# Fourth and sixth chunk of batches 1 to 7: computed key pairs ahead of fetched ones

## Chip, core and metric

One core of a Trainium2 chip. The metric is the device time of one execution in microseconds (us); the kernel before takes 2296.9 us (median of three runs, 2296.57 to 2297.46).

## What is computed

For 8 batches of 3200 rows, an attention without softmax and a gated unit behind it:

```
scores = (1/S) * z @ z.T          # z: 3200 x 64
attn   = relu(scores) ** 2        # symmetric
x      = u * (attn @ v)           # u, v: 3200 x 256
gate   = sigmoid(causal conv of x over 5 rows)
out    = ((x @ w_val) * gate) @ w_out
```

Every product is made of three matmuls of fp32r parts (high by high, high by low, low by high).

## The kernel before

**Tiling.** The 25 tiles of 128 rows of a batch are taken in seven chunks of queries (4, 4, 4, 4, 3, 3, 3 tiles; in the last batch 4, 4, 4, 4, 4, 3, 2). I call them c0 to c6 here, so the fourth and sixth are c3 and c5. Against each chunk stand 13 pairs of key tiles, numbered 0 to 12; the last "pair" is a single tile. One chunk with one pair is a step; all steps stand in one list (`steps`), sorted by batch, chunk and `place`, the pair's position in its chunk. I write c3 p5 for the step at place 5 of c3.

**Three kinds of pairs.** `attn` is symmetric, so a block whose keys belong to an earlier chunk was already computed, with the roles exchanged. `turn` (L419, L429) transposes such a block on DVE, `keep` (L441) stores it in DRAM, `m_fetch` (L450, L456) loads it again into one of four `m` buffers. Such a pair is *fetched* (`mirrored` in the code). Other pairs are *computed*: `scores` on PE into PSUM, Relu and Square on ACT (L501, L502). Two pairs are mixed: `halves` (half of a diagonal block is fetched) and `split` (one of two tiles is fetched). Each kind ends alike: a cast on ACT makes the high part `ah` (L504), a subtraction on DVE the low part `al` (L510; L491 for mixed pairs).

**What PE does in a step.** `attend` multiplies `ah`, `al` of the step's pair by `v`. Scores are made three steps ahead (`AHEAD`). If the pair three steps ahead is not fetched, the step runs in *half rows*: `attend` (L338, through `side_by_side`) cuts each matmul in two of 64 rows that run beside each other, and the scores (contraction 64) go between its two parts. Otherwise the step runs in *whole rows*: `attend_whole` (L544), with no scores. The same choice is made for the work that is tied to a chunk's places: `project` or `project_whole` (L700) of the chunk before the last at p0, and `value` or `value_whole` (L652) of the last chunk at p5.

**What sets the order.** Python loops write each engine's order out by hand. `todo` holds the rest of the work by step: `BEHIND` the gated unit of the chunk before (at p9 `gate_value(1)` on DVE, L664; at p10 `gate_value_high(1)` on ACT, L668; at p11 `gate_value_low(1)` on DVE, L673, whose result `gvl` the projection at the next p0 reads), `u_prep` (L563), `x_low` (L601), and `z_order` (L226), two ACT copies that put a chunk's queries into block order in the single buffer `zq`. In a step, PE's work comes first, then `todo`, then `weights_of` for the pair three ahead; the subtraction and turn of a step p11 wait until `gated` (L574), which needs the chunk's last matmul.

Of the kernel before, what the change touches and what calls it, by code (L numbers as in the profile page):

```python
# [13 lines left out]
BLK = 32  # L14
# [3 lines left out]
def attn_glu_kernel(  # L18
# [30 lines left out]
    B, S, D = u.shape  # L49
# [8 lines left out]
    n_chunks = -(-NT // 4)  # L58
# [4 lines left out]
    i = even.index(base) if extra < n_chunks else None  # L63
# [4 lines left out]
    all_firsts = [[sum(sz[:i]) for i in range(n_chunks)] for sz in all_sizes]  # L68
# [146 lines left out]

    zq = {}

    def has_copy(b, c):

        return c < n_chunks - 1 and b > 0  # L220

    def z_order(b, c, x):
# [11 lines left out]
    pairs = [(k, min(2, NT - k)) for k in range(0, NT, 2)]  # L234
    NP = len(pairs)

    def two_pairs(b, c):

        first = all_firsts[b][c]
        return all_sizes[b][c] == 4 and first % 2 == 0 and first < NT // 2 + 2 and (b > 0 or c > 1)  # L240

    def own(b, c, x):
        return all_firsts[b][c] // 2 + x

    place = {}
    for b in range(B):
        for c in range(n_chunks):
            order = list(range(NP))
            if two_pairs(b, c):
                order.append(order.pop(own(b, c, 1)))  # L250
            if b == B - 1 and c == n_chunks - 1:
                new = [i for i in order if sum(pairs[i]) > all_firsts[b][c]]
                order = new + [i for i in order if i not in new]
            for p, i in enumerate(order):
                place[b, c, i] = p
# [74 lines left out]
    def side_by_side(upper, lower):  # L330


        ins = None
        for i in range(max(len(upper), len(lower))):
            for r, mms in zip(rows, (upper, lower)):
                if i < len(mms):
                    out_, st, mv, first, last = mms[i]
                    ins = nc.tensor.matmul(out_, st[r], mv[r], start=first, stop=last)  # L338
        return ins
# [24 lines left out]
    def scores(b, c, i, terms=range(3)):  # L364
        k, n = pairs[i]
        w = all_sizes[b][c] * P
        if (b, c, i) not in st_:
            st_[b, c, i] = ps.tile([P, 2, 512], F32, name="s", bufs=2)
        s = st_[b, c, i]

        q = zt[b, c][:, :, :w].rearrange("p x (t a r) -> p x a t r", t=all_sizes[b][c], r=BLK)
        if has_copy(b, c):
            q = zq[b, c][:, :, :w].rearrange("p x (a y) -> p x a y", a=P // BLK)
        if halves(b, c, i):
            q, w = q[:, :, :, 2 * BLK :] if has_copy(b, c) else q[:, :, :, 2:], w // 2
        a = P // BLK
        sides = []
        for j in range(2):

            one_tile = n == 1 or split(b, c, i)  # L380
            g, t = all_homes[b][k + (n - 1 if one_tile else j)]
            ks = slice(t * P, (t + 1) * P)
            qs = slice(j * (a // 2), (j + 1) * (a // 2)) if one_tile else slice(0, a)
            kk = zt[b, g]
            mms = []
            for m in terms:
                kp, qp = ((0, 1), (1, 0), (0, 0))[m]
                mms.append((s[:, j, : w // 2 if one_tile else w], kk[:, kp, ks], q[:, qp, qs], m == 0, m == 2))
            sides.append(mms)
        side_by_side(*sides)  # L390
# [8 lines left out]
    def halves(b, c, i):  # L399
        return two_pairs(b, c) and i == own(b, c, 1)  # L400

    def split(b, c, i):

        (j, g, *_), *more = runs(b, i)
        return bool(more) and more[0][1] == c and keeps(b, g, c) and (b, c) != (B - 1, n_chunks - 1)

    def mirrored(b, c, i):
        return all(keeps(b, all_homes[b][t][0], c) for t in range(pairs[i][0], sum(pairs[i])))
# [326 lines left out]
    AHEAD = 3  # L735
    FETCH = 3
    VALUE = 5

    def project_at(b, c):

        return 2 if (b, c) == (0, 2) else 0
# [5 lines left out]
    def at_step(s, fn, *args, first=False):  # L747
        work = todo.setdefault(min(s, END), [])
        work.insert(0 if first else len(work), (fn, args))

    def start(b, c):
        return (b * n_chunks + c) * NP
# [29 lines left out]
    for b in range(B):  # L782
        for c in range(n_chunks):
            s0 = start(b, c)
            nxt = s0 + NP
            for h in range(DH):
                for part in range(2):
                    at_step(max(s0 + U_LOAD[b > 0][c], 2) + 2 * h + part, u_load, b, c, h, part)
            if (b, c) != LAST:
                for r, fn, args in BEHIND:  # L790
                    at_step(nxt + r, fn, b, c, *args)
                for x in range(DH):
                    at_step(nxt + project_at(*steps[nxt][:2]) + 1 + x, out_copy_before, b, c, x)
            at_step(max(s0 + U_PREP[b > 0][c], 6), u_prep, b, c)

            met = start(b, 0) + all_firsts[b][c] // 2 - AHEAD
            if has_copy(b, c):
                for x in range(2):
                    at_step(s0 - (5 if c == 0 else 3), z_order, b, c, x)
            if b == 0:  # L800
                met -= c == 1
                at_step(met - 5, z_load, b, c)
                early = 1 if c == 0 else 0
                at_step(met - 3 - early, z_turn, b, c)
                at_step(met - 2 - early, z_high, b, c)
                at_step(met - 1 - early - (c >= 2), z_low, b, c)
            else:
                s1 = Z_FROM[b][c] + start(b - 1, 4)
                at_step(s1, z_load, b, c)
                late = 1 if b == 1 else 0  # L810
                at_step(s1 + late + 3, z_turn, b, c)
                at_step(s1 + late + 4, z_high, b, c)
                at_step(s1 + late + 5, z_low, b, c)
            for i in range(NP):
                if mirrored(b, c, i) or halves(b, c, i) or split(b, c, i):
                    at_step(s0 + place[b, c, i] - AHEAD - FETCH, m_fetch, b, c, i, first=True)
        if b == 0:
            for i in range(NP):
                at_step(i - 3, v_high, b, i)
                at_step(i - 2 if i else -3, v_low, b, i)  # L820
            for g in range(n_chunks):
                at_step(all_firsts[b][g] // 2 - 5, v_load, b, g)
        else:
            s, kept_at, loads = start(b - 1, 1) + 2, {}, []
            for g in range(n_chunks):
                load_at = s - 5
                for t in range(0, all_sizes[b][g], 2):
                    at_step(s, v_make_high, b, g, t)
                    at_step(s + 1, v_make_low, b, g, t)
                    at_step(s + 2, v_keep, b, g, t)  # L830
                    for k in range(t, min(t + 2, all_sizes[b][g])):
                        kept_at[(all_firsts[b][g] + k) // 2] = s + 5
                    s += 5
                loads.append((load_at, v_load, b, g))
                s += 2
            for i in range(NP):
                at_step(max(start(b, 0) - NP + i + 2, kept_at[i]), v_fetch, b, i)
            for load in loads:
                at_step(*load)
# [8 lines left out]
    with tc.manual_schedule():  # L848
        zeros = sb.tile([P, CW], F32R, name="zeros", tag="gvl", bufs=1)
        nc.vector.memset(f32(zeros), 0.0)  # L850
        for s in range(min(todo), END + 1):
            b, c, i = steps[s] if s >= 0 else (0, 0, 0)
# [51 lines left out]
            if s == END:  # L904
# [4 lines left out]
                b, c = LAST  # L909
# [66 lines left out]
```

## Time and profile before

| | |
|---|---|
| median of three runs | 2296.9 us |
| the profiled execution's own time | 2296.48 us |
| its span in the trace | 2294.7 us |
| PE matmul busy | 2287.3 us, 100% of the span |
| PE weight load busy | 88% |
| DVE busy | 79% |
| ACT busy | 77% |
| DMA engines | 76.3% on the main queue, 203 GB/s |
| granted TensorE clock | full in all 40 slices of the page |

Busy times of PE overlap (matmuls are pipelined), so a matmul's price is read from the distance between starts, not from its duration. Times in rows are us from the span's start. The batches 1 to 6 repeat each other closely, so batch 3 is shown: c2 runs from 961.6, c3 from 1007.2, c4 from 1051.5, c5 from 1086.0 and c6 from 1119.5.

### The profile page before, as it was taken

How to read it: one execution, taken by the hardware profiler on the slowest of the kernel's cores; microseconds unless marked ns; L12 is line 12 of the kernel's file. 1: busy time of each engine (PE TensorE's matmuls, PEld its weight loads, DVE VectorE, ACT ScalarE, POOL GpSimd, SP SyncE). 2: the span in 40 equal slices, each digit the busy share in tenths (PEclk: the TensorE clock that was granted, in tenths of full speed). 3: DMA queues.
4: the chain of work that ended last, by engine and by line, in shares of the span. 5: the costliest groups of instructions: out<-in, count | busy, mean ns of one | idle time of the engine just before them, and what ended most of it. 6: DMA issues, size and time to landing. Idle time of an engine off the chain costs nothing.

```text
span 2294.7 us, 47249 instructions
## 1 busy us (share of the span) xinstructions
PE 2287.3 (100%) x18629; PEld 2009.2 (88%) x18629; DVE 1817.6 (79%) x2391; ACT 1777.5 (77%) x2402; POOL 54.7 (2%) x108
## 2 busy tenths in 40 slices
PE   9999999999999999999999999999999999999999
PEld 8788988889888998889988899888998889988889
DVE  8777788788878878788788887888877887778776
ACT  8988788776888768887688776887768876687765
POOL 0000000000000000000000000000000000000000
PEclk9999999999999999999999999999999999999999
DMA  6265797778977889688987789878897788966653
GB/s 133 65 157 149 211 265 201 200 205 247 255 182 202 215 242 252 170 213 221 241 238 192 197 227 248 224 189 213 235 232 213 203 223 228 256 172 170 187 164 91
DMA packets 688576, 466.39 MB, mean 203 GB/s; under 512 B 355297, under 2 KB 639201, under 8 KB 688353
## 3 DMA queue, kind: packets, MB, share of 16 engines
q1 hardware_dynamic: 687296, 463.23, 76.3%
q8 instruction: 146, 2.39, 0.4%
q14 instruction: 78, 0.63, 0.1%
q10 hardware_dynamic: 1056, 0.13, 0.0%
HBM read 251.73 MB, written 211.48 MB: 202 GB/s over the span
## 4 chain that ended last, share of the span: by engine, by line
PE 94%; ACT 2%; SPq 1%; DVE 1%; issue 1%; DMA 1%; ACTq 0%; DVEq 0%
PE acc L338 44%; PE acc L544 28%; PE s L338 10%; PE misc L338 6%; PE misc L700 4%; PE misc L652 1%; SPq L166 1%; ACT a L502 1%; ACT a L501 1%; ACT ah L504 0%; SPq L280 0%; DMA m<-mir 0%; DVE gvl L673 0%; DVE al L510 0%; DMA u_raw<-in_u_dram 0%
## 5 line engine op out<-in xcount | busy, mean ns | idle before, releaser
L338 PE MATMUL acc<-ah,v_hl 64*128 64x512 f32 (+1 forms) x6632 | 1074.3, 375 | 0.6 <-DVE v_hl L296 0.6
L338 PEld LDWEIGHTS acc<-ah,v_hl 64*128 64x128 f32 x6632 | 623.3, 184 | 110.6 <-issue 11.8
L544 PE MATMUL acc<-ah,v_hl 128*128 128x384 f32 (+2 forms) x2284 | 638.6, 355 | 0.1
L338 PE MATMUL acc<-al,v_hl 64*128 64x512 f32 (+1 forms) x3316 | 628.2, 374 | 0.0
L510 DVE TENSOR_TENSOR al<-a,ah 128x1024 fp32r<-128x1024 f32 (+3 forms) x388 | 424.1, 1093 | 222.8 <-ACT ah L504 215.0
L501 ACT ACTIVATE a<-s 128x1024 f32<-128x1024 f32 (+3 forms) x388 | 357.2, 921 | 152.2 <-PE s L338 149.1
L544 PEld LDWEIGHTS acc<-ah,v_hl 128*128 128x128 f32 x2284 | 416.8, 188 | 47.4 <-ACT a L474 6.4
L510 DVE TENSOR_TENSOR al<-m,ah 128x768 fp32r<-128x768 f32 (+2 forms) x303 | 307.8, 1023 | 121.9 <-ACT ah L504 121.2
L544 PE MATMUL acc<-al,v_hl 128*128 128x384 f32 (+2 forms) x1142 | 402.2, 352 | 0.1
L502 ACT ACTIVATE a<-a 128x1024 f32<-128x1024 f32 (+3 forms) x388 | 372.3, 960 | 12.3
L504 ACT CAST ah<-m 128x768 fp32r<-128x768 f32 (+2 forms) x303 | 267.1, 892 | 146.7 <-DMA m<-mir 111.0
L338 PEld LDWEIGHTS acc<-al,v_hl 64*128 64x128 f32 x3316 | 314.2, 184 | 45.4
L504 ACT CAST ah<-a 128x1024 fp32r<-128x1024 f32 (+3 forms) x350 | 333.6, 953 | 11.1
L419 DVE STREAM_TRANSPOSE turned<-a 128x1024 f32<-128x1024 f32 (+3 forms) x318 | 320.0, 1011 | 22.3 <-DMA mir<-turned 21.2
L615 DVE SCALAR_TENSOR_TENSOR gate<-x,cw,gate 128x512 f32<-128x512 f32 (+2 forms) x448 | 303.3, 677 | 4.5 <-ACT gate L613 0.3
L338 PE MATMUL s<-zq,zhl 64*128 64x512 f32 (+3 forms) x2052 | 259.8, 356 | 0.0
L544 PEld LDWEIGHTS acc<-al,v_hl 128*128 128x128 f32 x1142 | 214.8, 188 | 15.1 <-DVE al L510 0.3
L338 PEld LDWEIGHTS s<-zq,zhl 64*128 64x128 f32 x2052 | 185.4, 184 | 29.5
L620 ACT ACTIVATE gate<-gate 128x512 f32<-128x512 f32 (+2 forms) x112 | 65.4, 584 | 43.3 <-DVE gate L615 43.1
L574 DVE TENSOR_TENSOR x<-acc,ut 128x512 f32<-128x512 f32 (+2 forms) x112 | 67.4, 629 | 39.4 <-PE acc L338 25.2
L668 ACT CAST gvh<-gv 128x512 fp32r<-128x512 f32 (+2 forms) x112 | 64.0, 572 | 26.6 <-DVE gv L664 26.4
L304 ACT CAST v_made<-v_raw 128x512 fp32r<-128x512 f32 x97 | 55.9, 576 | 36.5 <-DMA v_kept<-v_made 35.4
(116 smaller groups left out, 2018.2 us busy)
## 6 DMA issues: line engine op xcount, KB each, us to landing
m<-mir SPq DMA_DIRECT2D x191, 384.0 KB, 4.9
mir<-turned SPq DMA_DIRECT2D x340, 192.0 KB, 3.9
mir<-turned SPq DMA_DIRECT2D x188, 256.0 KB, 4.3
m<-mir SPq DMA_DIRECT2D x94, 512.0 KB, 6.0
v_hl<-v_kept SPq DMA_DIRECT2D x84, 512.0 KB, 6.7
v_kept<-v_made SPq DMA_DIRECT2D x71, 512.0 KB, 5.4
u_raw<-in_u_dram SPq DMA_DIRECT2D x264, 64.0 KB, 3.3
out_dram<-ob SPq DMA_DIRECT2D x33, 512.0 KB, 4.0
```

Of the source, the lines that this page charges most:

```text
L338: ins = nc.tensor.matmul(out_, st[r], mv[r], start=first, stop=last)
L419: nc.vector.transpose(into[:, t : t + m], a[:, j * w : (j + m) * w].rearrange("p (t m x) -> p t m x", t=m, x=BLK))
L501: nc.scalar.activation(a.rearrange("p (j x) -> p j x", j=2), s[:, :, :each], AF.Relu, scale=scale)
L502: nc.scalar.activation(a, a, AF.Square)
L504: nc.scalar.copy(hi, a)
L510: nc.vector.tensor_tensor(lo, a, f32(hi), op=ALU.subtract)
L544: nc.tensor.matmul(out_, st, mv, start=first, stop=last)
L574: nc.vector.tensor_tensor(x[:, h, HALO : HALO + w], accs[b, c][h][:, :w], ut[b, c][:, h, :w], op=ALU.mult)
L615: nc.vector.scalar_tensor_tensor(g, tap, cw[:, h, k : k + 1], g, op0=ALU.mult, op1=ALU.add)
L620: nc.scalar.activation(g, g, AF.Sigmoid)
L668: nc.scalar.copy(gvs[b, c][0][:, e, :w], gv_[b, c, e][:, :w])
L700: nc.tensor.matmul(out_, st, mv, start=first, stop=last)
```

## The change

For c3 of batches 1 to 7 and c5 of batches 1 to 6 (`new_first`), the places are given anew: computed pairs first (in c5 the split pair last of them), fetched pairs behind. c3 was 0 1 2 3 4 5 | 6 8 9 10 11 12 7 and is 6 8 9 10 11 12 7 | 0 1 2 3 4 5; c5 was 0 to 8 | 9 10 11 12 and is 10 11 12 9 | 0 to 8. Since c4 and c6 begin with fetched pairs, and c2 and c4 end with computed ones, the stretches run together. Three things follow. The queries of c3 and c5 are needed in order earlier, so `z_order` moves from three steps ahead of the chunk to five. The single `zq` is then no longer the previous chunk's at that chunk's last place, so its last pair reads the queries unordered. And the fetch of c3's `halves` pair is made one step later, after its store.

```diff
-    def has_copy(b, c):
-
+    def has_copy(b, c, i=None):
+        if i is not None and new_first(b, c + 1) and place[b, c, i] == NP - 1:
+            return False
         return c < n_chunks - 1 and b > 0
...
+    def new_first(b, c):
+        return b > 0 and c % 2 == 1 and 1 < c < n_chunks - (2 if b == B - 1 else 1)
...
+            if new_first(b, c):
+                new = [i for i in order if sum(pairs[i]) > all_firsts[b][c]]
+                new.sort(key=lambda i: pairs[i][0] < all_firsts[b][c])
+                order = new + [i for i in order if i not in new]
...
-        if has_copy(b, c):
+        if has_copy(b, c, i):
             q = zq[b, c][:, :, :w].rearrange("p x (a y) -> p x a y", a=P // BLK)
...
-                    at_step(s0 - (5 if c == 0 else 3), z_order, b, c, x)
+                    at_step(s0 - (5 if c == 0 or new_first(b, c) else 3), z_order, b, c, x)
...
-                    at_step(s0 + place[b, c, i] - AHEAD - FETCH, m_fetch, b, c, i, first=True)
+                    at_step(s0 + place[b, c, i] - AHEAD - FETCH + (new_first(b, c) and halves(b, c, i)), m_fetch, b, c, i, first=True)
```

**PE, from c2 p9 to c2 p10 of batch 3**, before (v_hl10 and v_hl11 are the pairs 10 and 11; s is a block of scores):

```order
L338 MATMUL acc1_13281<-al_13626,v_hl10_11979 128x512
L338 MATMUL acc0_13280<-ah_13625,v_hl10_11979 128x512
L338 MATMUL acc1_13281<-ah_13625,v_hl10_11979 128x512
L544 MATMUL acc0_13280<-ah_13677,v_hl11_12120 128x512
L544 MATMUL acc0_13280<-al_13678,v_hl11_12120 128x512
L544 MATMUL acc0_13280<-ah_13677,v_hl11_12120 128x512 x2
```

And in the change, where the same step goes on in half rows, with scores of c3 (zhl3 and zq) between its parts:

```order
L350 MATMUL acc0_13330<-ah_13675,v_hl10_12029 128x512
L350 MATMUL acc1_13331<-ah_13675,v_hl10_12029 128x512
L350 MATMUL acc0_13330<-ah_13725,v_hl11_12170 128x512
L350 MATMUL acc1_13331<-ah_13725,v_hl11_12170 128x512
L350 MATMUL acc0_13330<-al_13726,v_hl11_12170 128x512
...
L350 MATMUL s_13848<-zq_13770,zhl3_11109 128x512 x6
L350 MATMUL acc1_13331<-ah_13725,v_hl11_12170 128x512
```

The switch to whole rows at c2 p10 is gone; it comes after c3 p3 now.

**ACT, from c4 p8 to c4 p10 of batch 3**, before (a<-s is the Relu of a computed pair, ah<-m the cast of a fetched one, zq<-zhl5 is `z_order` of c5, gvh is `gate_value_high(1)`):

```order
L620 ACTIVATE gate_22108<-gate_22108 128x512
L501 ACTIVATE a_22430<-s_22397 128x768
L502 ACTIVATE a_22430<-a_22430 128x768
L504 CAST ah_22428<-a_22430 128x768
L501 ACTIVATE a_22475<-s_22449 128x384
L502 ACTIVATE a_22475<-a_22475 128x384
L504 CAST ah_22473<-a_22475 128x384
L668 CAST gvh_22315<-gv_22471 128x512
L226 CAST zq_22496<-zhl5_19240 128x384 x2
L504 CAST ah_22506<-m_22368 128x4x2x96
```

And in the change:

```order
L632 ACTIVATE gate_22214<-gate_22214 128x512
L229 CAST zq_22525<-zhl5_19340 128x384 x2
L513 ACTIVATE a_22535<-s_22501 128x768
L514 ACTIVATE a_22535<-a_22535 128x768
L516 CAST ah_22533<-a_22535 128x768
L513 ACTIVATE a_22578<-s_22554 128x384
L514 ACTIVATE a_22578<-a_22578 128x384
L516 CAST ah_22576<-a_22578 128x384
L680 CAST gvh_22421<-gv_22574 128x512
L513 ACTIVATE a_22628<-s_22596 128x768
L514 ACTIVATE a_22628<-a_22628 128x768
L516 CAST ah_22626<-a_22628 128x768
```

The two copies stand ahead of the Relu of place 11, and where one cast of a fetched pair followed `gvh`, three instructions of c5's first computed pair follow it.

## Rows read from the trace of the kernel before

**Rows 1.** PE's waits in the whole span: total us, times, longest us

```profile
PE misc L700 <- DVE gvl L673: 0.3, 1, 0.3
```

**Rows 2.** PE timeline, half to whole, c2 p9/p10: start, us, line, tiles, shapes, count

```profile
999.96 0.39 PE L338 MATMUL acc<-ah,v_hl 64*128 64x512 f32 x2
1000.28 0.50 PE L544 MATMUL acc<-ah,v_hl 128*128 128x512 f32 x1
...
1003.38 0.39 PE L544 MATMUL acc<-al,v_hl 128*128 128x512 f32 x1
```

**Rows 3.** PE timeline, twelve whole-row matmuls amid a stretch, c3 p1 to p2

```profile
1014.67 0.61 PE L544 MATMUL acc<-ah,v_hl 128*128 128x512 f32 x2
...
1017.39 0.61 PE L544 MATMUL acc<-ah,v_hl 128*128 128x512 f32 x2
```

**Rows 4.** PE timeline, whole to half, c3 p2/p3

```profile
1018.07 0.39 PE L544 MATMUL acc<-ah,v_hl 128*128 128x512 f32 x1
1018.38 0.50 PE L338 MATMUL acc<-ah,v_hl 64*128 64x512 f32 x2
...
1019.88 0.86 PE L338 MATMUL s<-zq,zhl 64*128 64x512 f32 x6
```

**Rows 5.** PE timeline, whole to half at 384 columns, c5 p5/p6

```profile
1101.73 0.33 PE L652 MATMUL misc<-xh,w_val_lo 128*128 128x384 f32 x1
...
1103.63 0.34 PE L652 MATMUL misc<-xh,w_val_hi 128*128 128x384 f32 x1
1103.90 0.44 PE L338 MATMUL acc<-ah,v_hl 64*128 64x384 f32 x2
```

**Rows 6.** PE timeline, projection in whole rows at c5 p0

```profile
1086.04 0.28 PE L700 MATMUL misc<-w_out_hi,gvl 128*128 128x256 f32 x1
...
1086.63 0.28 PE L700 MATMUL misc<-w_out_hi,gvh 128*128 128x256 f32 x1
1086.98 0.39 PE L700 MATMUL misc<-w_out_hi,gvl 128*128 128x256 f32 x1
```

**Rows 7.** PE timeline, projection in half rows at c1 p0: nine pairs of matmuls

```profile
916.17 0.28 PE L338 MATMUL misc<-w_out_hi,gvl 64*128 64x256 f32 x2
...
917.24 0.39 PE L338 MATMUL s<-zq,zhl 64*128 64x512 f32 x2
```

**Rows 8.** ACT timeline, c4 p8 to c5 p0

```profile
1078.12 0.80 ACT L501 ACTIVATE a<-s 128x768 f32<-128x768 f32 x1
...
1083.15 0.62 ACT L668 CAST gvh<-gv 128x512 fp32r<-128x512 f32 x1 [1.00 <-DVE gv L664]
1083.67 0.93 ACT L226 CAST zq<-zhl 128x384 fp32r<-128x384 f32 x2
1084.50 0.83 ACT L504 CAST ah<-m 128x768 fp32r<-128x768 f32 x1
```

**Rows 9.** DVE timeline, c4 p8 to c5 p0

```profile
1080.69 0.96 DVE L510 TENSOR_TENSOR al<-a,ah 128x768 fp32r<-128x768 f32 x1 [0.56 <-ACT ah L504]
...
1082.46 0.65 DVE L664 TENSOR_TENSOR gv<-misc,gate 128x512 f32<-128x512 f32 x1
...
1085.37 0.96 DVE L510 TENSOR_TENSOR al<-m,ah 128x768 fp32r<-128x768 f32 x1 [0.71 <-ACT ah L504]
1086.24 0.68 DVE L673 TENSOR_TENSOR gvl<-gv,gvh 128x512 fp32r<-128x512 f32 x1
```

**Rows 10.** DVE timeline, the `gvl` that the projection at c3 p0 reads

```profile
1005.03 0.69 DVE L673 TENSOR_TENSOR gvl<-gv,gvh 128x512 fp32r<-128x512 f32 x1
```

**Rows 11.** DVE timeline in c5 p1: `x_low` and, after `u_prep`, the next subtraction

```profile
1091.58 0.95 DVE L601 TENSOR_TENSOR xl<-x,xh 128x768 fp32r<-128x768 f32 x1
...
1093.35 0.92 DVE L510 TENSOR_TENSOR al<-m,ah 128x768 fp32r<-128x768 f32 x1
```

**Rows 12.** Windows, c6: length, busy us by engine (PE first), clock, DMA share, GB/s

```profile
1119.51:1153.03 33.52, 33.52 (x266) 32.86 (x266) 26.84 (x44) 20.50 (x33) 0.98 (x2) 1.00 1.04 270
```

**Rows 13.** The page's DMA issues, fetches of 384 KB: count, KB, median us

```profile
m<-mir SPq DMA_DIRECT2D x191, 384.0 KB, 4.9
```

More of the change, by code (lines that the diff above doesn't have):

```diff
@@ L371, in scores @@
         q = zt[b, c][:, :, :w].rearrange("p x (t a r) -> p x a t r", t=all_sizes[b][c], r=BLK)
-        if has_copy(b, c):
+        if has_copy(b, c, i):
             q = zq[b, c][:, :, :w].rearrange("p x (a y) -> p x a y", a=P // BLK)
         if halves(b, c, i):
-            q, w = q[:, :, :, 2 * BLK :] if has_copy(b, c) else q[:, :, :, 2:], w // 2
+            q, w = q[:, :, :, 2 * BLK :] if has_copy(b, c, i) else q[:, :, :, 2:], w // 2
         a = P // BLK
```

## The prediction

> **What bounds the kernel now.** I read the list of PE's waits first, then PE's timeline by the distance of starts, and only then the engines that feed PE. The page has PE busy for 100% of the span, and past batch 0 the list of waits names nothing but a projection that waits 0.3 us for `gvl` [rows 1]; batch 3 shows such a gap at c5 p0, between 1086.63 and 1086.98 [rows 6]. So the kernel is PE's issue, step after step, and a gain has to come out of the distances between PE's starts. In a stretch of whole rows, twelve matmuls of 512 columns take 2.72 us, 0.227 each [rows 3]; at 384 columns eleven take 1.90 us, 0.173 each [rows 5]. A pair of half-row matmuls costs the same as one whole-row matmul. What stands out are the switches between the two: the starts around them are further apart.
>
> **What a switch costs.** Half to whole at 512 columns: the last pair starts 0.32 us before the first whole-row matmul, 0.09 over the pitch, and the next 13 take 3.10 us instead of 2.95 [rows 2, 3]: 0.24. Whole to half: 0.31 at the border, 0.08 over, then six pairs in 1.50 us instead of 1.36 [rows 4]: 0.22. At 384 columns the border is 0.27 against 0.173, 0.10 over [rows 5]; I take the tail of 0.12 that it has from the 512 rows, so 0.22 each way. A stretch of whole rows costs its two switches: 0.46 us at 512, 0.44 at 384.
>
> **What the change removes.** In each of batches 1 to 7 the stretch at the border of c2 and c3 melts into that of c3 and c4 (512 columns), and in batches 1 to 6 that of c4 and c5 into that of c5 and c6 (384). The kinds of pairs are as many as before, so half and whole steps are too. Gone are 7 x 0.46 + 6 x 0.44 = 5.9 us, all of it on PE's path.
>
> **What it moves on PE.** The projections at c3 p0 and c5 p0 go from whole to half rows. Five whole-row matmuls take 0.59 us [rows 6], nine half-row pairs 1.07 [rows 7]: 0.118 against 0.119. But half rows put a score group amid the projection, where the row widths change twice more; I price that between 0 and 0.1 us (a switch's border), 0.05 each, 13 times 0.05 = 0.7 us back. The value matmuls of c3 go from half to whole at the same pitch: nothing. The unordered scores of a chunk's last pair (13 of them) show in no row; they are between 0 and 0.1 us as well, and I take nothing, since the same number of columns streams. PE alone would gain 5.2 us.
>
> **What it moves on the others.** The two `z_order` copies go ahead of the Relu of c4 place 11, and three instructions of a computed pair now stand between `gvh` and the subtraction that precedes `gvl`. This is the place that decides, because PE already waits there. Before: Relu of place 11 at 1078.12, its subtraction at 1080.69, `gv` at 1082.46, `gvh` at 1083.15, the copies at 1083.67, the cast of c5's first pair at 1084.50, its subtraction at 1085.37, `gvl` from 1086.24 to 1086.92 [rows 8, 9]. No engine has slack in this chain: ACT goes from one cast to the next until place 12, and DVE takes `gv` behind the turn of place 11. In the change the copies push the Relu, and everything to `gvh`, by their 0.83 us (1083.67 to 1084.50): `gvh` at 1083.98. After it (0.52) comes a Relu, and from a Relu to its subtraction it is 2.57 us (1078.12 to 1080.69), so that starts at 1087.07, and `gvl` 0.87 behind it at 1087.94: 1.70 later than before.
>
> The projection starts later too: c4 p10 to p12 now carry scores, two groups of three pairs at 0.173 and one half as wide, 1.3 us, less the switch of 0.22 that goes: 1.1 us. So PE waits about 0.6 longer than before, on top of the 0.35 - 0.12 = 0.23 us at the seventh matmul [rows 6]. In half rows the seventh pair is again the first to read the late part. Six times 0.55 (between 0.5 and 0.6) is 3.3 us given back. Bounds: at best the old wait goes too (0.3 each, 1.9 gained), at worst the whole 1.70 counts, as if the projection started no later (10 us); I stay with the chain, whose every link has a row.
>
> At c3 p0 the same chain has room: `gvl` starts at 1005.03 [rows 10], done 0.69 later, 1.5 us ahead of the projection, with which c3 starts at 1007.2. It moves by some 2.6 (the same three ACT instructions at 1024 elements, with the copies now ahead of a place that is a single tile), the projection by 1.8: 0.7 are left. Nothing is charged.
>
> The fetches of c5 move four places back, so twenty fetched pairs follow each other to c6 p10. A buffer comes back every four steps, 4 x 12 x 0.173 = 8.3 us, against 4.9 for the landing [rows 13], 0.83 for the cast and 0.96 for the subtraction [rows 8, 9]: 6.7. Hidden, with 1.6 us to spare a turn. SP's queue has the store of c5's turned blocks, which waits for the turn of c5's third pair, ahead of the fetch for p7; by the line of DVE's work under the second rival that is some 7 us into c5, and p7 comes some 20 us into it.
>
> **Sum.** -5.9 + 0.7 + 3.3 = -1.9. The profiled execution took 2296.48 us, which would make 2294.6; the median of the runs is 0.4 above it, so I predict **2295.0**. A measurement of this kernel can tell about 0.2%, 4.6 us; the forecast lies inside that.
>
> **Rivals.**
>
> *PE gets its gain (faster).* If the copies found idle time on ACT after all, or the wait at c5 p0 stayed as it is, -5.2 remains: 2291.7; with that wait gone, 2289.8. For it: after place 12 ACT idles 1.00 us for `gv` [rows 8]. Against it: that idle time is itself made by DVE's chain, which moves along. 0.13.
>
> *DVE's queue at c5 p1 to p4 (slower).* Behind the late `gvl`, DVE has `gated`, the subtraction and turn of places 1 and 2, two subtractions of the split pair, then `x_low` and `u_prep`, 1.77 us [rows 11], and only then the subtraction that c5 p4 needs, while PE runs whole steps of 2.08. Adding these from `gvl`'s end (1088.6, with one wait for a cast of place 1) I get that subtraction done at 1098.5, and PE at c5 p4 at 1098.8. It decides from 0.3 us of further lateness in the line; at 1.5 us it costs 1.2 a batch, 7.2 in all: 2302. It speaks against it that such lateness needs several links to be off one way. 0.18.
>
> *The twenty fetches (slower).* DMA is full in c6, busy share 1.04 at 270 GB/s [rows 12], and the fetches of c5 now press toward it. From a landing of 6.5 us a turn of the four buffers exceeds 8.3; at 8 us each step loses 0.4, and after the 3 us that are in hand twelve steps lose 2 us, 12 in all: 2307. 0.05.
> The Trainium skill ("Perfetto Trace Analysis", Roofline) puts the limit of one core's 16 DMA engines at about 435 GB/s. By that rule c6 would have a third of its DMA to spare and this rival no chance; the trace disagrees, with the engines busy throughout at 270, so it keeps its 0.05, and the sum is the same either way.
>
> *The change does nothing to the switches.* The listing of the order shows them gone; below 0.01.
>
> **How the numbers follow.** The forecast, inside 0.2%, has 0.63; faster 0.13 for the first rival and 0.01 of the forecast's edge; of the slower rivals' 0.23 some 0.02 ends inside the band. So faster 0.14, same 0.65, slower 0.21. The forecast's own range is 2292.5 to 2298 (the wait from 0.1 to 1.1 more per batch). For 8 in 10 it is widened to 2291.5, where the first rival's nearer case lies, and to 2300.5, half the way into the DVE rival.
>
> **What would show it.** PE's timeline at c2 p10 and c3 p3 keeps its pitch; c2 and c3 together are 0.4 us shorter. At c5 p0 the seventh pair of the projection starts some 0.8 us late instead of 0.23, with `gvl` ending near 0.6 later against the projection's start than before; c4 and c5 together stay within 0.2 us of their old length. DVE's subtraction of c5 place 4 ends just ahead of PE. I am wrong if the seventh pair starts on time (then 2291.7 or less), if a second gap stands at c5 p3 or p4, or if the waits for fetched pairs grow until PE shows them in c6.

## The result, and the profile after

The changed kernel takes 2308.3 us (median of five runs, 2305.1 to 2310.8), the kernel before 2296.8 in the same session: 1.0048 times as long, 95% interval 1.0036 to 1.0059. That is 11.4 us slower; I had predicted 2295.0, with 2300.5 as the upper end. The profiled execution took 2305.11, its span is 2303.3 against 2294.7, at the same granted clock of 1.0; it is the shortest of the five, so some 3 us of the median lie in no trace.

PE's waits in the changed kernel (total us, times, longest us), beside [rows 1]:

```profile
PE misc L350 <- DVE gvl L685: 6.0, 9, 1.2
PE acc L556 <- DVE al L522: 2.4, 4, 0.9
```

The entry for `gvl` grew, as I had said it would at c5 p0, but it has nine waits and not six. A new entry names `al`, the low part of a fetched pair, in whole rows. I take what each place costs from the distances of PE's starts, chunk by chunk, against the kernel before:

| Where | us, all batches | Foreseen |
|---|---|---|
| c2 and c3, where PE does not wait: 7 x 0.37 | -2.6 | -2.9 |
| c4 and c5, with the wait at c5 p0: 6 x 0.41 | +2.5 | +1.0 |
| c3 p8 to p12, waits for fetched pairs (1.8, 2.4, 0.8, 0.7, 0.5, 0.3 in batches 1 to 6) | +6.4 | 0 |
| c0 p0, waits for `gvl` (0.9 and 1.4 in batches 3 and 6) | +2.3 | 0 |
| ahead of the first moved step: batch 0 (-0.8), and c0 p0 of batch 1, the ninth wait for `gvl` (+0.9) | +0.1 | 0 |
| c6 of batches 6 and 7 | -0.1 | 0 |

The sum is 8.6, and so is the difference of the spans. Of the 11.2 us that are lost in rows two to four, 8.7 stand in places that the prediction charged with nothing. The fifth row is scatter between executions: no step in it is moved.

**The foreseen wait.** PE's timeline at c5 p0 of batch 3 in the changed kernel, the projection in half rows; [rows 6] are the same place before:

```profile
1093.48 0.28 PE L350 MATMUL misc<-w_out_hi,gvh 64*128 64x256 f32 x2
1094.38 0.39 PE L350 MATMUL misc<-w_out_hi,gvl 64*128 64x256 f32 x2 [0.62 <-DVE gvl L685]
1094.60 0.28 PE L350 MATMUL misc<-w_out_lo,gvh 64*128 64x256 f32 x2
...
1095.18 0.25 PE L350 MATMUL s<-zq,zhl 64*128 64x192 f32 x2
1095.41 0.39 PE L350 MATMUL misc<-w_out_hi,gvl 64*128 64x256 f32 x2
1095.63 0.28 PE L350 MATMUL misc<-w_out_lo,gvh 64*128 64x256 f32 x2
```

The seventh pair starts 0.90 us after the sixth, where 0.12 is the pitch: 0.78 late, with "some 0.8" foreseen. Its second cost is the 0.22 behind it, 0.10 over the pitch. The score group amid the projection adds another 0.10 (1095.41 to 1095.63) besides its own border. The chain that makes `gvl` late, ACT first, then DVE, beside [rows 8, 9]:

```profile
1083.79 0.91 ACT L229 CAST zq<-zhl 128x384 fp32r<-128x384 f32 x2
1084.61 0.81 ACT L513 ACTIVATE a<-s 128x768 f32<-128x768 f32 x1
...
1089.65 0.62 ACT L680 CAST gvh<-gv 128x512 fp32r<-128x512 f32 x1 [1.00 <-DVE gv L676]
1090.17 0.81 ACT L513 ACTIVATE a<-s 128x768 f32<-128x768 f32 x1
```

```profile
1087.19 0.96 DVE L522 TENSOR_TENSOR al<-a,ah 128x768 fp32r<-128x768 f32 x1 [1.39 <-ACT ah L516]
...
1088.96 0.65 DVE L676 TENSOR_TENSOR gv<-misc,gate 128x512 f32<-128x512 f32 x1
...
1092.76 0.96 DVE L522 TENSOR_TENSOR al<-a,ah 128x768 fp32r<-128x768 f32 x1 [1.60 <-ACT ah L516]
1093.64 0.68 DVE L685 TENSOR_TENSOR gvl<-gv,gvh 128x512 fp32r<-128x512 f32 x1
```

Copies 1083.79, Relu 0.82 behind, subtraction 2.58 behind that, `gvh` at 1089.65, a Relu 0.52 later, its subtraction 2.59 later, `gvl` 0.88 later: each link is the one that the prediction drew.

**The new wait in c3.** PE's timeline, whole rows of batch 2, the second matmul of c3 p9 and of c3 p11:

```profile
760.60 0.50 PE L556 MATMUL acc<-al,v_hl 128*128 128x512 f32 x1 [0.60 <-DVE al L522]
...
767.42 0.50 PE L556 MATMUL acc<-al,v_hl 128*128 128x512 f32 x1 [0.70 <-DVE al L522]
```

SP's queue ahead of it, the same batch (start, us from the first issue to the last, queue, line, tiles, count; m is a fetch, mir the store of a turned block):

```profile
722.09 14.05 SPq L453 DMA_DIRECT2D mir<-turned  x12
736.30 0.71 SPq L462 DMA_DIRECT2D m<-mir  x1
737.05 0.82 SPq L468 DMA_DIRECT2D m<-mir  x1
737.92 3.90 SPq L166 DMA_DIRECT2D z_raw<-in_z_dram  x4
741.92 3.22 SPq L453 DMA_DIRECT2D mir<-turned  x4
745.18 0.84 SPq L468 DMA_DIRECT2D m<-mir  x1
...
749.39 0.47 SPq L332 DMA_DIRECT2D v_kept<-v_made  x1
```

and what SP waited for between 722 and 739 us:

```profile
SPq L453 <- DVE turned L431: 4.9, 1, 4.9
SPq L453 <- DVE turned L441: 2.6, 1, 2.6
```

SP takes 14.05 us for twelve pieces, the stores of three blocks, 7.5 of them waiting for c3's own blocks: 2.6 for the diagonal block (`turn` at L441), then 4.9 for the block that c4 will fetch (L431). Until DVE has turned it, it stands in front of the queue, and the fetches behind it wait too. The fetch for c3 p8 stands in the program at step p2, which PE begins at 738.11; it leaves at 745.18. The fetches are then late up to p12. The wait for the L431 block alone does not set the loss: by the same list it is 3.8 to 5.2 us in each of batches 1 to 7, and PE loses 2.4 us in batch 2 and nothing in batch 7.

### The profile page after: what moved, and what is told of

The parts are those of the page before. It is cut to its first block, busy times and chain, and to the rows that moved or that the text cites. A ratio compares the mean times of both kernels' runs of the same rounds, so it can differ in the third digit from the quotient of the medians.

```text
span 2303.3 us, 47573 instructions
## 1 busy us (share of the span) xinstructions
PE 2287.0 (99%) x18779; PEld 2009.4 (87%) x18779; DVE 1819.4 (79%) x2391; ACT 1776.6 (77%) x2402; POOL 48.8 (2%) x108
## 3 DMA queue, kind: packets, MB, share of 16 engines
q1 hardware_dynamic: 687296, 463.23, 77.6%
## 4 chain that ended last, share of the span: by engine, by line
PE 79%; ACT 7%; DVE 6%; DMA 4%; issue 2%; SPq 1%; DVEq 0%; ACTq 0%
PE acc L350 37%; PE acc L556 23%; PE s L350 9%; PE misc L350 6%; PE misc L712 3%; ACT a L514 2%; ACT a L513 2%; PE misc L664 2%; ACT ah L516 1%; DVE al L522 1%; DMA mir<-turned 1%; DVE turned L431 1%; DMA z_raw<-in_z_dram 1%; DMA m<-mir 1%; SPq L166 1%
## 5 line engine op out<-in xcount | busy, mean ns | idle before, releaser
L350 PE MATMUL acc<-ah,v_hl 64*128 64x512 f32 (+1 forms) x6528 | 1057.6, 376 | 0.4 <-DVE v_hl L308 0.4
L350 PEld LDWEIGHTS acc<-ah,v_hl 64*128 64x128 f32 x6528 | 613.3, 185 | 105.6 <-issue 9.2
L556 PE MATMUL acc<-ah,v_hl 128*128 128x384 f32 (+2 forms) x2336 | 650.4, 355 | 0.1
L350 PE MATMUL acc<-al,v_hl 64*128 64x512 f32 (+1 forms) x3264 | 618.5, 374 | 0.0
L556 PEld LDWEIGHTS acc<-ah,v_hl 128*128 128x128 f32 x2336 | 426.4, 188 | 44.2 <-ACT a L485 3.7
L556 PE MATMUL acc<-al,v_hl 128*128 128x384 f32 (+2 forms) x1168 | 413.8, 354 | 2.9 <-DVE al L522 2.4
L350 PEld LDWEIGHTS acc<-al,v_hl 64*128 64x128 f32 x3264 | 309.1, 185 | 45.1
L431 DVE STREAM_TRANSPOSE turned<-a 128x1024 f32<-128x1024 f32 (+3 forms) x318 | 320.5, 1012 | 24.5 <-DMA mir<-turned 23.5
L556 PEld LDWEIGHTS acc<-al,v_hl 128*128 128x128 f32 x1168 | 219.7, 188 | 23.9 <-DVE al L522 8.3
L350 PEld LDWEIGHTS s<-zq,zhl 64*128 64x128 f32 x1974 | 180.1, 185 | 28.3
```

Of the source, the lines that this page charges most:

```text
L431: nc.vector.transpose(into[:, t : t + m], a[:, j * w : (j + m) * w].rearrange("p (t m x) -> p t m x", t=m, x=BLK))
L556: nc.tensor.matmul(out_, st, mv, start=first, stop=last)
```

## Experiments

Four theories. **Q**: SP issues in order, and a store of c3's turned blocks that waits for DVE holds the fetches behind it. **S**: the loss lies in the sixth chunk. **A**: the wait at c5 p0 comes from the two `z_order` copies and the computed pair ahead of `gvl`. **B**: the DMA engines are full where fetches follow each other, whoever issues them. Times of the kernel before in the four sessions: 2296.8, 2297.0, 2296.8, 2296.5.

**One chunk at a time.** In `new_first`:

```diff
-        return b > 0 and c % 2 == 1 and 1 < c < n_chunks - (2 if b == B - 1 else 1)
+        return b > 0 and c == 3                # first run
+        return 0 < b < B - 1 and c == 5        # second run
```

> Only the fourth chunk (c3) is reordered. Theory Q (SP's queue at c3 holds the fetches of the pairs that now come last behind stores that wait for DVE): PE gains 0.37 us a batch from the switches, 2.6 in all, and loses the waits that the changed kernel's trace has at c3 p8 to p12, 6.4 us and up to 9: 2300 to 2304 us. Rival S (the loss is all in the sixth chunk): 2294.2.

Measured 2307.0, ratio 1.0048 (1.0031 to 1.0065). The c3 part alone costs nearly as much as the whole change, more than the 2300 to 2304 expected, and the waits for `al` are more, "5.4, 11, 0.7" where the change has "2.4, 4, 0.9". By the distances of starts c3 loses 11.6 us here, against 6.4 with both chunks reordered.

> Only the sixth chunk (c5) is reordered. Theory A (two ACT copies and a computed pair ahead of gvl make the projection at c5 p0 wait 0.8 us instead of 0.2) and the three waits of the projection at c0 p0 that the changed kernel's trace has (3.2 us): 2296.8 + 2.4 + 3 = 2302. If c5 does no harm, it keeps the 2.7 of its switches: 2294.

Measured 2305.8, ratio 1.0046 (1.0031 to 1.0061). So S falls: each half costs about as much as both together. In c4 and c5 it has the same +0.4 a batch; the rest of its loss stands at c0 p0 (1.1, 1.6 and 1.6 us in batches 3 to 5). In both profiles batch 0, where no step is moved, is 0.6 to 0.7 us longer than before, in the changed kernel's 0.8 shorter; so differences of 1.4 us between single profiles can be scatter.

**The copies one step later**, in c5 alone:

```diff
-                    at_step(s0 - (5 if c == 0 or new_first(b, c) else 3), z_order, b, c, x)
+                    at_step(s0 - (5 if c == 0 or (new_first(b, c) and c == 3) else 4 if new_first(b, c) else 3), z_order, b, c, x)
```

> As the kernel with c5 alone, the two ACT copies of z_order one step later (c4 p9, behind the Relu of place 11 and ahead of that of place 12). Theory A: the Relu of place 11 is no longer pushed, gvl comes 0.8 us sooner and the wait at c5 p0 goes nearly to nothing: 4.5 us less than with c5 alone, about 2297.5. Rival (the three instructions of the computed pair make the delay, not the copies): at most 1 us less.

Measured 2299.3, ratio 1.001 (1.0001 to 1.002), 6.6 us less than with the copies early (3.9 by the two spans). c4 and c5 now lose nothing but gain 0.39 to 0.42 a batch, where no other wait stands in them: the wait at c5 p0 is gone. So of the two causes that A names the copies are enough, and the computed pair alone makes no wait. Losses of 0.3 to 1.3 us stay in single batches, at c5 p12, in c6 and at c0 p0.

**c3's stores one step later** in SP's queue, with c3 alone reordered. `keep` leaves a block of c3 for its next call:

```diff
-    mirror, m_in, turned_, to_keep = {}, {}, {}, []
+    mirror, m_in, turned_, to_keep, seen = {}, {}, {}, [], set()
...
-        while to_keep:
+        while to_keep and (to_keep[0][1] != 3 or to_keep[0][0] == 0 or to_keep[0] in seen):
             b, c, g = to_keep.pop(0)
...
+        seen.update(to_keep)
```

> As the kernel with c3 alone, each store of c3's turned blocks issued one step later, so that the fetches of the same step are ahead of it in SP's queue. Theory Q: the fetches of c3's places 7 to 12 are issued some us sooner, the waits at c3 p8 to p12 go, 2294 to 2296. Rival B (the DMA engines are full there, whatever the order): the same time as with c3 alone, 2300 to 2304.

Measured 2295.0, ratio 0.9993 (0.9984 to 1.0003): 12 us less than the same order with the stores early. SP's queue of this kernel at the same place (its step p2 begins at 735.74, 2.37 us earlier):

```profile
719.65 7.71 SPq L453 DMA_DIRECT2D mir<-turned  x8
...
729.82 2.74 SPq L166 DMA_DIRECT2D z_raw<-in_z_dram  x4
732.60 3.27 SPq L453 DMA_DIRECT2D mir<-turned  x4
735.91 0.85 SPq L469 DMA_DIRECT2D m<-mir  x1
...
741.34 0.57 SPq L332 DMA_DIRECT2D v_kept<-v_made  x1
```

and PE's waits in it:

```profile
PE misc L357 <- DVE zeros L863: 1.5, 1, 1.5
PE s L350 <- ACT a L514: 0.5, 1, 0.5
PE acc L350 <- DVE v_hl L308: 0.4, 1, 0.4
PE misc L713 <- DVE gvl L686: 0.3, 1, 0.3
```

The diagonal block's wait is still there (2.9 us of the 7.71), the one for the L431 block is not: its store now goes out at 732.60, behind two fetches (728.87 and 729.25). The fetch for p8 leaves 0.17 us after p2 begins, not 7.07; `al` is gone from the list. The windows from the start of c3 p2 to that of p12 of batch 2, of the changed kernel and of this one (length, busy us by engine, PE first, then clock, DMA share, GB/s):

```profile
738.11:770.07 31.96, 30.57 (x165) 24.00 (x162) 25.40 (x31) 18.40 (x27) 0.19 (x1) 1.00 0.93 239
```

```profile
735.74:765.31 29.57, 29.57 (x165) 24.28 (x161) 25.30 (x31) 18.67 (x28) 1.63 (x1) 1.00 0.95 246
```

The engines moved more per second where nothing waited, 246 against 239 GB/s. So B is not the cause in c3, and Q is: one step of delay of c3's stores takes the loss away, but for 0.2 us in batch 1.

**The whole change with c3's stores later.**

> The whole change, with each store of c3's turned blocks one step later in SP's queue. If the waits at c3 p8 to p12 come from SP alone (theory Q), the 6.4 us of excess of c3 in the changed kernel go: 2308.3 - 6.4 = 2301.9, PE's list of waits has no entry for a fetched pair (al) in c3, and what is left above the kernel before is the wait for gvl at c5 p0 (0.88 us in six batches) and that at c0 p0. The rival, that the two reordered chunks load the DMA engines together: 2305 or more, with al still in the list.

Measured 2302.5, ratio 1.0023 (1.0014 to 1.0032). c2 and c3 now keep -0.37 to -0.38 in every batch, c4 and c5 still lose 0.4, and c0 p0 1.0, 1.3 and 0.8 in batches 3, 4 and 6. The two `al` waits left are in c6 of batch 1.

**The turn of c6's queries.** In the changed kernel DVE, at the end of batch 2's c6, and PE behind it:

```profile
870.51 0.58 DVE L196 STREAM_TRANSPOSE zz<-z_raw 128x384 f32<-128x384 f32 x1 [2.65 <-DMA z_raw<-in_z_dram]
...
875.26 0.52 DVE L685 TENSOR_TENSOR gvl<-gv,gvh 128x384 fp32r<-128x384 f32 x1
```

```profile
875.83 0.39 PE L350 MATMUL misc<-w_out_hi,gvl 64*128 64x256 f32 x2 [0.60 <-DVE gvl L685]
```

DVE stands 2.65 us at a turn whose load has not landed, with the subtractions and `gvl` behind it. In the kernel before, that idle time is 0.86:

```profile
864.27 0.58 DVE L196 STREAM_TRANSPOSE zz<-z_raw 128x384 f32<-128x384 f32 x1 [0.86 <-DMA z_raw<-in_z_dram]
```

So theory Z: this turn makes the wait at c0 p0. The other batches bear it out. In the changed kernel and the one with c5 alone the turn waits 2.5 to 3.3 us at the end of c6 in five batches, and behind these five c0 p0 loses 0.9 to 1.6 us; where it waits 1.3 us or less in batches 1 to 6, the next c0 p0 loses nothing. SP's queue has the load of these queries, in the changed kernel and before:

```profile
861.85 4.05 SPq L166 DMA_DIRECT2D z_raw<-in_z_dram  x4
```

```profile
855.81 3.93 SPq L166 DMA_DIRECT2D z_raw<-in_z_dram  x4
```

It leaves 20.65 us into c6 (from 841.20), where it left 19.00 us into c6 before (from 836.81), and its first piece lands in 6.7 us, before in 7.4. So in batch 2 the load was issued late and did not land more slowly. In all five batches it leaves 20.6 to 21.1 us into c6 (before: 18.7 to 19.0) and lands in 6.4 to 8.2 us (before: 6.5 to 7.5). In batch 6 it leaves as late or later, but lands in 5.5 us or less, and nothing is lost. What held SP's queue back there was not followed.

The experiment, with c5 alone and its copies later:

```diff
-                late = 1 if b == 1 else 0
+                late = 1 if b == 1 else 3 if c == n_chunks - 1 else 0
                 at_step(s1 + late + 3, z_turn, b, c)
```

> The sixth chunk alone, copies one step later (2299.3 as it stood), and the turn of c6's queries three steps later on DVE. If that turn, waiting on DVE for its transfer, is what makes gvl late for the projection at c0 p0 (theory Z), the gaps at c0 p0, 3.7 us in the profiled run, go: 2295.6. The rival, that the late gvl comes from ACT's or DVE's own work or from the fetched pairs at the end of c6: the gaps stay, 2299.

Measured 2298.0, ratio 1.0003 (0.9994 to 1.0012). In the trace PE waits for no `gvl` at c0 p0 any more, so Z has its place right; the medians differ by 1.2 us only, within the two intervals, and losses at c6 p5 (1.0 and 1.3 us in batches 2 and 3) and c0 p4 (1.4 in batch 1) stand elsewhere.

**c5's stores later.** The same edit of `keep` for c5, without the later turn:

> The sixth chunk alone, copies one step later, and each store of c5's turned blocks one step later in SP's queue. If the store of c5's blocks, waiting for DVE, holds the fetches behind it as at c3 (theory Q), the gaps at c5 p12 and c6 p5, 2.8 us in the profiled run, go: 2296.5, with no wait for al in PE's list. The rival, that transfers in c5 and c6 land late because the DMA engines are full (theory B): 2299, the gaps stay.

Measured 2301.3, ratio 1.002 (1.0011 to 1.0029). A miss: gaps at c5 p12 and c6 p5 stay (0.3 to 1.0 us, in batches 3, 5 and 6), and those at c0 p0 are up to 1.7. What was right for c3 takes nothing away in c5: the time is 2.0 us above that with the stores early.

**All three remedies on the whole change**, with c5's stores later and without:

> The whole change with all three remedies: stores of c3's and c5's turned blocks one step later, copies of c5 one step later, the turn of c6's queries three steps later. If the causes are these and add up, PE keeps 0.37 us a batch at c2 and c3 (seven) and 0.42 at c4 and c5 (six): 2.6 + 2.5 below the kernel before, 2291.7, and PE's list of waits past batch 0 is empty. If DMA load takes part in it, gaps stay in c5, c6 or at c0 p0: 2294 to 2298.

> The whole change with three remedies, but the stores of c5 where the change has them: stores of c3's turned blocks one step later, copies of c5 one step later, the turn of c6's queries three steps later. The stores of c5 made no gain in the sixth chunk alone. If they have no part in it, 2294 to 2295.5 as with them; if SP's queue in c5 matters once the rest is mended, gaps return at c5 p12 and c6 p5: 2297 or more.

Measured 2295.1, ratio 0.9988 (0.9979 to 0.9997), and 2294.3, ratio 0.9991 (0.9982 to 1.0000). The first one falls short of the sum that was expected, 2291.7, and lies where its rival put it, 2294 to 2298. Its profile is one of its shortest executions, a span of 2291.4 against 2294.7: 3.3 us, not 5.1. c2 and c3 keep 0.37 in six of seven batches, c4 and c5 0.40 in five of six, but PE still waits 0.4 us for `al` at c3 of batch 1 and 0.3 for `gvl` at c0 p0 there, and 0.4 to 0.5 are lost in c6 of batch 2 and c5 of batch 6. Other executions are up to 3.7 us longer. The second one's profile shows what a longer execution has: 1.7 and 1.2 us at c0 p4 in batches 1 and 2, 1.2 at c6 p5 in batch 6. At c0 p4 the trace names the wait. DVE stands at a turn whose buffer's last stores have not landed; they left at 594.95 to 597.75 and landed up to 602.41:

```profile
602.53 1.25 DVE L431 STREAM_TRANSPOSE turned<-a 128x1024 f32<-128x1024 f32 x1 [4.39 <-DMA mir<-turned]
```

In this kernel and in the one with c6's turn later, that wait is 4.3 to 4.9 us in the three batches where c0 p4 loses 1.2 to 1.7; where it is 3.4 or less (1.3 to 2.6 in the kernel before), PE loses 0.4 at most. c5's stores make no difference that shows. These are the best versions found, with the c3-only kernel and its later stores; all three are about 0.1% below the kernel before, and only for the first does the whole interval lie below 1.

**Loads on POOL's queue.** To part Q from B in c5 and c6, `z_load` and `v_load` of batches 1 to 7 issue from POOL, which has next to nothing to do:

```diff
-            queues=(nc.sync, nc.scalar) if b == c == 0 else (nc.sync,),
+            queues=(nc.sync, nc.scalar) if b == c == 0 else (nc.gpsimd,) if b else (nc.sync,),
...
-            nc.sync.dma_start(
+            (nc.gpsimd if b else nc.sync).dma_start(
                 v_raw[b, g][a * BLK : (a + 1) * BLK, :n, :],
```

> The sixth chunk alone, copies one step later (2299.3 as it stood), and the loads of queries and values of batches 1 to 7 (z_raw, v_raw) issued from POOL's queue instead of SP's: the same bytes, fewer issues between the fetches. If SP's queue of issues holds the fetched pairs in c5 and c6 (theory Q), the gaps at c5 p12, c6 p5 and c0 p0 go and PE keeps its 0.42 us in six batches: 2294.3. If the DMA engines are full there whoever issues (theory B): 2298 to 2300, with al and gvl still in PE's list. If POOL is slow at issuing these loads, z_raw lands later and the gaps at c0 p0 grow: over 2300.

> The whole change with the three remedies (2295.1) and the loads of queries and values on POOL's queue. Theory Q: the last gaps go, 2.6 + 2.5 us below the kernel before: 2291.9. Theory B: no change, 2295. POOL slow: over 2297.

> The kernel before with the loads of queries and values on POOL's queue, nothing else. It has no wait for a fetched pair, so theories Q and B both expect no change, 2297.0 within 1; if POOL is slow at issuing, the projections at c5 p0 and c0 p0 show it and it is slower.

Measured 2299.8 (ratio 1.0013, 1.0004 to 1.0022), 2306.4 (1.0043, 1.003 to 1.0056) and 2306.0 (1.004, 1.0027 to 1.0053). The control decides how to read them: the move alone makes the kernel before 9 us slower, with new waits in PE's list of that run:

```profile
PE misc L338 <- DVE gvl L673: 3.9, 4, 1.1
...
PE acc L338 <- DVE al L510: 1.1, 3, 0.5
```

So these three runs do not part Q from B. In the first of them c5 p12 and c6 p5 are clean in all batches, which speaks for SP's part there; but waits at c0 p0 (1.2 to 1.4 us in four batches) and c6 p10 came in their place. In the second the waits at c3 p11 and p12 are back.

## Why the prediction was wrong

**The step that failed** is the one on the fetches. It asked of c5 whether twenty fetched pairs find their buffers in time ("Hidden, with 1.6 us to spare a turn") and whether a store stands ahead of one of them in SP's queue. For c3, which is moved in the same way, it read only `gvl` and closed with "Nothing is charged". There the queue was the limit: computed pairs now come first in c3, so their turned blocks are stored just ahead of the fetches of the same chunk, and the store of the first block for c4 waited 4.9 us for DVE at the front of the queue. Measured: 6.4 us in the profile, and 12 us between the two kernels that differ in these stores alone. The Trainium skill ("DMA: Bandwidth & Descriptors", Anatomy of one DMA — SWDGE (gpsimd) path) says that a DMA's semaphore wait is spent on the issuing sequencer, before dispatch. That section describes the path of POOL's queue; the 4.9 us on SP's queue agree with it, and the sentence, read for c3 too, would have pointed at the place.

**Second, c0 p0 was in no term.** The prediction had the fetches of c5 press toward c6, where DMA is full (the window below, beside [rows 12]: share 1.06 at 273 GB/s), and looked for the harm at fetched pairs. What came late was the load of queries in c6, which DVE waits for ahead of `gvl`. The harm moved through DVE to a projection: 2.3 us.

```profile
1125.56:1159.08 33.52, 33.52 (x265) 32.87 (x266) 25.64 (x41) 20.85 (x33) 0.98 (x2) 1.00 1.06 273
```

**Third, a mis-sized term.** The projection in half rows was priced at 0.05 a chunk, between 0 and 0.1. The scores of c5's split pair, three pairs of matmuls, stood in one group before, at c5 p6:

```profile
1105.05 0.47 PE L338 MATMUL s<-zq,zhl 64*128 64x192 f32 x6
1105.36 0.36 PE L338 MATMUL acc<-ah,v_hl 64*128 64x384 f32 x2
1105.56 0.33 PE L338 MATMUL acc<-al,v_hl 64*128 64x384 f32 x2
```

That is 0.31, and 0.03 over the pitch in the pair behind. Now they stand at c5 p0 in two parts. One pair goes amid the projection (1095.18 to 1095.41 above, 0.23, and 0.10 over the pitch behind it), two go into the product with `v` that follows, here in the kernel with all three remedies and c5's stores later:

```profile
1090.89 0.36 PE L350 MATMUL s<-zq,zhl 64*128 64x192 f32 x4
1091.11 0.45 PE L350 MATMUL acc<-ah,v_hl 64*128 64x384 f32 x2
1091.40 0.34 PE L350 MATMUL acc<-al,v_hl 64*128 64x384 f32 x2
```

0.22, and 0.12 over. The two parts cost 0.67 where the one group cost 0.34, so the term is 0.33 a chunk. It closes the sum in c4 and c5 where nothing waits: -0.41 for the two switches by the same distances, +0.33 for this, -0.33 because the old wait of [rows 6] is gone (0.23, and 0.10 in the pair behind it) make -0.41, and 0.39 to 0.42 is measured. Six times the missing 0.28 is 1.7 us, and 1.5 lie between the 1.0 foreseen and the 2.5 measured. The price could be read before: at c1 p0, behind the rows of [rows 7], the first pair after the score group takes 0.22 (917.47 to 917.69), not 0.12.

**What was right.** The switches: 0.37 a batch in c2 and c3, 0.41 foreseen (0.46 less 0.05), in every batch without a wait (batch 7 of the changed kernel, batches 2 to 7 with c3's stores later). The wait at c5 p0: 0.33 before and 0.88 now, 0.55 more, as predicted. One row was read for another: the 0.3 us of [rows 1] stand in batch 0, at 237.59 us, and past batch 0 PE's list of waits is empty. The gap of [rows 6], on which the working rests, is there all the same. At c3 p0 `gvl` ended at 1013.45, the projection began at 1014.33: 0.88 us of room, 0.7 foreseen. None of the rivals came as written. The DVE queue at c5 p1 to p4 shows no gap in any batch. The third one had the time nearly right, 2307, by luck, and the wrong mechanism: it wanted landings of 6.5 us in c6. Its fetches in batches 1 to 6 have a median of 5.2 us, before 5.5, and over the whole kernel it is 5.2 as well, beside 4.9 in [rows 13]:

```profile
m<-mir SPq DMA_DIRECT2D x191, 384.0 KB, 5.2
```

PE waits for no fetched pair in c6 of the profiled execution.

**What stays open.** Why c3's waits shrink from batch to batch and are absent in batch 7, while SP's wait for DVE stays near 5 us, was not tried; nor why they cost nearly twice as much with c3 alone. Nor is it settled what makes pairs late at c5 p12 and c6 p5, and stores land late ahead of c0 p4, in some executions: SP's order or full engines. They come and go in single batches, and they may be why the best versions gain 2 us in the median where the profile of one gains 3.3; the other executions left no trace.

## What to carry to other kernels

A reordering that is right for PE also rewrites every in-order queue that feeds it: list, for each moved step, which stores now stand ahead of which fetches, and when the engine that each store waits for is done. Do this for every place that the change touches, not for the one that looks tightest, and then move the waiting entry behind the ones that could go. And price a removed switch against the borders that the new order makes: here 0.33 of the 0.41 us that the two switches were worth at c5 went back to a score group that now stands in two parts.

## What the runs showed of the hardware that was not expected

One waiting issue delays work of quite another kind: the cast of a value tile on ACT at 754.12, behind the late store of `v_kept` (749.39), kept ACT from the cast of c3 p8, whose fetch had landed at 751.08:

```profile
754.12 0.62 ACT L316 CAST v_made<-v_raw 128x512 fp32r<-128x512 f32 x1 [3.40 <-DMA v_kept<-v_made]
754.64 1.05 ACT L516 CAST ah<-m 128x1024 fp32r<-128x1024 f32 x1
```

And the queue that a load is issued from changes its transfers. The page's table of DMA queues (packets, MB, share of 16 engines) for the kernel before with its loads on POOL:

```profile
q1 hardware_dynamic: 569024, 428.80, 68.8%
q0 software_dynamic: 15616, 34.43, 5.8%
```

The 34.4 MB went in 15616 packets, 2.2 KB each on average, where SP's queue, with these loads still on it, has 687296 packets in that table: the same bytes took 118 thousand, 0.3 KB each. The engines' time on both queues is 74.6% of the span together, against 76.3% on SP's queue alone, and yet the kernel was 9 us slower and its 384 KB fetches landed later, 5.4 us against 4.9: what POOL's issue saves SP does not show in the time. The Trainium skill ("Trainium Kernel Development and Optimization", Key Constraints) says that issuing from several engines saves only the sequencer's issue time, since all share the same DMA engines; here it cost 9 us, and which of the later landings came from the form of the transfers and which from their new place in time was not tried.
